# Loading the next batch's k, q and v between the weight tiles, with DMA issues in program order and a later start of its attention

## The chip, the core and the metric

The kernel runs on one core of a Trainium2 chip. The metric is the device time of one execution in microseconds, as the median of several runs. The engines are named as the profile names them: PE is TensorE (matrix products and transpositions), ACT is ScalarE, DVE is VectorE, POOL is GpSimd, and SP is SyncE, which here does nothing but issue DMAs. SPq is SP's instruction queue.

## What is computed

There are 8 batches of 8 heads, 576 positions, a head size of 64, and 32 pack vectors per head. Each batch goes through two attentions, first from the pack vectors to the sequence and then from the sequence to the packed result. A feed-forward layer with a softplus follows.

```
def sm_attn(qq, kk, vv):
    s = scale * qq @ kk.T;  s -= max(s);  a = exp(s)
    return (a / (sum(a) + 1e-09)) @ vv
p_packed = sm_attn(p, k, v)
out      = sm_attn(q, p_packed, p_packed)        # (8, 8, 576, 64)
x = out as (4608, 512)
h = x @ w_in                                     # w_in: 512 x 2048
g = max(h, 0) + log1p(exp(-|h|))
result = g @ w_out                               # w_out: 2048 x 512, float32
```

The two weight matrices arrive as 64-bit floating point numbers. The kernel makes 32-bit numbers of them on the chip, with integer operations.

## The kernel before

**Units.** The feed-forward part of a batch is cut into 16 units f of 128 columns of w_in (rows of w_out). The loop over `units` runs through all of them, batch after batch. Unit f has a first product `gemm1` (tiles `ph`, two halves c of 288 positions, 12 matrix products of 288 columns), the softplus on ACT (absolute value, exponential, logarithm) and DVE (`e`, line 624), and a split of the result into a high and a low part on DVE (`gh`, `gl`, lines 611 and 612). The second product `gemm2_tile` (12 products of 512 columns into four accumulators `acc`) comes two units later (LAG = 2). Two `ph` banks exist for each pair of halves in turn, so the first product of unit f+1 waits until DVE has read `ph` of unit f.

**The factored first product.** The second attention's product with the packed vectors is not formed. `make_m` multiplies the packed vectors (`pt`) with columns of w_in (tiles `psm`, then `mh` and `ml`), and `gemm1` multiplies these with the attention weights `at_h` and `at_l`. In batch 0 one `make_m` serves two units: `psm` number c needs w_in's column tiles 2c and 2c+1, and it stands on PE two units ahead of its use, after the second products of the unit that is then in hand.

**Weight conversion.** `convert` goes through 32 tiles in the order i0, i1, o0, o1, i2, i3, o2, o3 and so on (i for w_in, o for w_out), so tile n = 12 is i6 and n = 24 is i12. For each: a DMA of 512 KB into a tile x (lines 149 to 157; two DMAs for an i tile, one for an o tile), two passes on ACT (`m`, line 196, and `r`, line 200), two on DVE (`t`, lines 202 and 207), and an addition on POOL (line 215). For an i tile the addition writes w_in's columns. For an o tile ACT copies the sum to `wo_h` (line 234) and DVE forms `wo_l` (line 240). From n = 8 on there are two x tiles in turn, so the load of tile n+2 waits until ACT has read tile n. There is one tile `m` in the main loop, so line 196 of tile n+1 waits until DVE has done line 207 of tile n. `conv` is advanced by CONV = 1.6 steps per quarter unit in batch 0.

**The next batch's attention.** `attention(b + 1)` is a generator that runs beside the units of batch b. It is advanced by PACE = 0.56 steps per quarter of a unit, from the batch's first quarter on, and what is left of it is run in unit 15. Its first step transposes k on DVE (`quads`, tiles `T_k`, line 252), and `scores1` multiplies the result with the pack vectors on PE (tiles `ps1`, line 276). q is transposed some steps later (`T_q`). k, q and v of the next batch are issued from within these generators: batch 1's k and v from `attention_first(0)`, and each batch's q from `attention_next` of its own.

**What sets the order.** PE's instructions stand in the order of the program. Those of the other engines, SP's DMA issues among them, are put in order by a scheduler that works with the program's priorities and its own view of durations. Each engine then runs its list strictly in order, so an instruction that waits holds up all that stand behind it. The k and q tiles share two buffers (tag `kq`), v has two of its own.

Of the kernel before, what the change touches and what calls it, by code (L numbers as in the profile page):

```python
# [9 lines left out]
F32 = mybir.dt.float32  # L10
# [16 lines left out]
def pack_attention_then_softplus_ffn(  # L27
# [14 lines left out]
    P = 128  # L42
# [3 lines left out]
    C = S // 2  # L46
    G = H * J // P
    HG = H // G
    NF = DFF // P
    NT = S // P  # L50
    REST = S - NT * P
    LAG = 2
    MC = 512
    Q = 32
    FIRST = 1
    scale = 1.0 / math.sqrt(D)

    const = ctx.enter_context(tc.tile_pool(name="const", bufs=1))
    ld = ctx.enter_context(tc.tile_pool(name="ld", bufs=G))
    cv = ctx.enter_context(tc.tile_pool(name="cv", bufs=1))  # L60
# [56 lines left out]
    def load(nm, b, g):  # L117
        if b >= B:
            return
        src = {"q": q, "k": k, "v": v}[nm][b, g * HG:(g + 1) * HG]  # L120
        if b < FIRST:
            if nm == "v":
                t = ld.tile([NP, HG, SI, D], F32, tag="v", name=f"{nm}_{b}_{g}")
            else:
                o = DFF - (["k", "q"].index(nm) * G + g + 1) * SI * D
                t = w_in_sb[:NP, :, o:o + SI * D].rearrange("x h (s d) -> x h s d", d=D)
            nc.sync.dma_start(
                t.rearrange("x h s d -> x h (s d)"),
                src.rearrange("h (x s) d -> x h (s d)", s=SI),
            )  # L130
        elif nm == "v":
            t = ld.tile([NP, HG, SI, D], F32, tag="v", name=f"{nm}_{b}_{g}")
            nc.sync.dma_start(
                t.rearrange("x h (m c) d -> x (h m) (c d)", c=2),
                src.rearrange("h (m x c) d -> x (h m) (c d)", x=NP, c=2),
            )
        else:
            t = ld.tile([P, HG, C], F32, tag="kq", name=f"{nm}_{b}_{g}")
            by_quad = src.rearrange("h (n x c) (e d) -> c e x (h n) d", x=Q, c=2, d=Q)
            for i in range(P // Q):  # L140
                nc.sync.dma_start(
                    t[i * Q:(i + 1) * Q].rearrange("x h (n d) -> x (h n) d", d=Q),
                    by_quad[i // 2, i % 2],
                )
        loaded[nm, b, g] = t
# [224 lines left out]
    def attention_first(b):  # L370


        a1 = [work.tile([P, S], F32, tag="a1", name=f"a1_{b}_{g}") for g in range(G)]
        pp = [None] * G
        kT, qT = [], []
        kt = turned("k", b, 0)
        for hh in range(HG):
            kT.append(transposed("k", b, 0, hh, kt))
            yield
        for c in range(2):  # L380
            scores1(b, 0, c, kT, a1[0])
        yield
        nm = softmax1_max(b, 0, a1[0])
        kt = turned("k", b, 1)
        kT = [transposed("k", b, 1, 0, kt)]
        yield
        z0 = softmax1_exp(b, 0, a1[0], nm)
        kT.append(transposed("k", b, 1, 1, kt))
        yield
        rs0 = softmax1_sum(b, 0, z0)  # L390
        for hh in range(2, HG):
            kT.append(transposed("k", b, 1, hh, kt))
            yield
        for c in range(2):
            scores1(b, 1, c, kT, a1[1])
        yield
        nm = softmax1_max(b, 1, a1[1])
        a1T = work.tile([NP, SI, P], F32, tag="a1T", name=f"a1T_{b}_0", bufs=1)
        for c in range(2):
            a1_transposed(b, 0, c, a1[0], a1T)  # L400
            yield
            if c == 0:
                z1 = softmax1_exp(b, 1, a1[1], nm)
        rs1 = softmax1_sum(b, 1, z1)
        pp[0] = packed(b, 0, a1T, rs0)
        load("k", b + 1, 0)
        yield
        qt = turned("q", b, 0)
        qT.append(transposed("q", b, 0, 0, qt))
        yield  # L410
        a1T = work.tile([NP, SI, P], F32, tag="a1T", name=f"a1T_{b}_1", bufs=1)
        for c in range(2):
            a1_transposed(b, 1, c, a1[1], a1T)
            yield
        res[b]["pt"].append(packed_transposed(b, 0, pp[0]))
        yield
        qT.append(transposed("q", b, 0, 1, qt))
        yield
        pp[1] = packed(b, 1, a1T, rs1)
        load("k", b + 1, 1)  # L420
        yield
        for hh in range(2, HG):
            qT.append(transposed("q", b, 0, hh, qt))
            yield
        load("v", b + 1, 0)
        a2 = scores2(b, 0, 0, qT)
        a2n = scores2(b, 0, 1, qT)
        yield
        softmax2_exp(b, 0, 0, a2)
        res[b]["pt"].append(packed_transposed(b, 1, pp[1]))  # L430
        yield
        qt = turned("q", b, 1)
        qT = [transposed("q", b, 1, 0, qt)]
        softmax2_div(b, 0, 0, a2)
        a2 = a2n
        yield
        qT.append(transposed("q", b, 1, 1, qt))
        softmax2_exp(b, 0, 1, a2)
        yield
        qT.append(transposed("q", b, 1, 2, qt))  # L440
        yield
        qT.append(transposed("q", b, 1, 3, qt))
        softmax2_div(b, 0, 1, a2)
        yield
        load("v", b + 1, 1)
        a2 = scores2(b, 1, 0, qT)
        a2n = scores2(b, 1, 1, qT)
        yield
        softmax2_exp(b, 1, 0, a2)
        yield  # L450
        softmax2_exp(b, 1, 1, a2n)
        softmax2_div(b, 1, 0, a2)
        yield
        softmax2_div(b, 1, 1, a2n)
        yield

    def attention_next(b):
# [2 lines left out]
        a1 = [work.tile([P, S], F32, tag="a1", name=f"a1_{b}_{g}") for g in range(G)]  # L460
        kT = [quads("k", b, 0)]
        yield
        load("q", b, 0)
        kT.append(quads("k", b, 1))
        yield
        load("q", b, 1)
        yield
        for c in range(2):
            scores1(b, 0, c, kT[0], a1[0])
        yield  # L470
# [55 lines left out]
        yield  # L526
        softmax2_div(b, 1, 1, a2n)
        yield

    def attention(b):  # L530
        return attention_first(b) if b < FIRST else attention_next(b)
# [151 lines left out]
    for f in range(NF):  # L683
        if f % 2 == 0:
            order += [("i", f), ("i", f + 1)]
        order.append(("o", f))
    PACE = 0.56
    CONV = 1.6
    CONV_EARLY = 1.6
    CONV_STEP = 14  # L690
# [16 lines left out]
    due = 0.0  # L707
# [8 lines left out]
    spare.clear()  # L716
    cdue = 0.0
    gs, acc = {}, None
    units = [(b, f) for b in range(B) for f in range(NF)]
    ahead, chain, due = iter(()), iter(()), 0.0  # L720
    for u in range(len(units) + LAG):
# [25 lines left out]
        for t in range(NT):  # L747
            if u >= LAG:
                gemm2_tile(
                    acc[t], gh, gl, f2, slice(t * P, (t + 1) * P), f2 == 0, f2 == NF - 1  # L750
                )
                if f2 == NF - 1:
                    store(acc[t], [(0, b2, t * P, P)], f"{b2}_{t}")
            if u < len(units):
                due += PACE
                while due >= 1:
                    next(ahead, None)
                    due -= 1
                if b == 0:
                    cdue += CONV  # L760
                    while cdue >= 1:
                        next(conv, None)
                        cdue -= 1
            next(chain, None)
# [37 lines left out]
```

## Time and profile before

| | us |
|---|---|
| median of 3 runs (836.68 to 838.5) | 838.15 |
| the profiled execution | 836.29 |
| its span in the trace | 834.5 |
| from batch 0's first unit to batch 1's first unit (52.9 to 215.4) | 162.5 |
| of these, PE busy | 96.67 |
| from there to the end (seven batches of units) | 619.1 |
| of these, PE busy | 613.58 |

The profile is one execution. Busy times of PE include the overlap of the products' pipelined ends. "Idle before" is the time in which an engine's next instruction could not begin, and what it waited for. The granted clock is a share of 2.4 GHz: 1.00 is 2.4 and 0.50 is 1.2.

### The profile page before, as it was taken

To read this page: it belongs to the slowest core of one execution; us is meant where nothing else is said; L and a number is where in the kernel's file an instruction comes from. 1 tells how busy PE (TensorE), PEld (TensorE's weight loads), DVE (VectorE), ACT (ScalarE), POOL (GpSimd) and SP (SyncE) were. 2 spreads that over 40 slices of the span, in tenths; PEclk is the share of its full clock that TensorE was granted. 3 is DMA by queue.
4 is the path that set the end of the run, shared out by engine and by line. 5 is a ranking of instruction groups with operands and counts; after the bars stand their busy time and mean duration, and the time that the engine had idled before them with its cause. 6 is when DMAs were issued, how large, how long until landed. Compare 5 with 4: busy or idle time off the path is not lost.

```text
span 834.5 us, 14191 instructions
## 1 busy us (share of the span) xinstructions
PE 734.6 (88%) x5312; PEld 580.9 (70%) x5312; DVE 543.5 (65%) x1228; ACT 434.1 (52%) x1073; POOL 89.5 (11%) x166
## 2 busy tenths in 40 slices
PE   5636546537999999999999999999999999999997
PEld 3324434426777877788778877787878777888886
DVE  2684557565757785595758665877586756765544
ACT  5643555446665554455655625466546355555550
POOL 1220222132000000000000000000000000000110
PEclk9557788768999999999999999999999999999999
DMA  9781536264153113230523032212321100000002
GB/s 213 211 169 29 136 83 148 77 168 100 36 105 61 29 52 60 67 55 10 108 57 59 1 91 59 57 30 75 62 57 30 51 14 1 1 26 26 1 1 63
DMA packets 168244, 55.96 MB, mean 67 GB/s; under 512 B 134896, under 2 KB 161520, under 8 KB 168176
## 3 DMA queue, kind: packets, MB, share of 16 engines
q1 hardware_dynamic: 167904, 55.00, 29.8%
q8 instruction: 41, 0.67, 0.3%
q14 instruction: 27, 0.22, 0.1%
q10 hardware_dynamic: 272, 0.07, 0.0%
HBM read 45.61 MB, written 9.44 MB: 66 GB/s over the span
## 4 chain that ended last, share of the span: by engine, by line
PE 78%; DVE 9%; DMA 5%; ACT 4%; issue 2%; POOL 2%; SPq 0%; DVEq 0%; POOLq 0%; ACTq 0%
PE acc L635 39%; PE ph L597 25%; PE acc_m L635 4%; PE psm L560 4%; DMA x_o<-in_moe_w_out 2%; PE ps L276 2%; DVE t L207 2%; DMA x_i<-in_moe_w_in 1%; PE psp L319 1%; POOL t L215 1%; DVE t L202 1%; PE psa L309 1%; ACT m L196 1%; DMA out<-o 1%; DVE e L624 1%
## 5 line engine op out<-in xcount | busy, mean ns | idle before, releaser
L624 DVE SCALAR_TENSOR_TENSOR e<-ph,e 128x288 f32<-128x288 f32 x256 | 113.4, 452 | 161.7 <-ACT e L622 161.1
L635 PE MATMUL acc<-wo_h,gh 128*128 128x512 f32 x512 | 208.5, 407 | 0.0
L635 PE MATMUL acc<-wo_l,gh 128*128 128x512 f32 x512 | 201.5, 394 | 0.0
L635 PE MATMUL acc<-wo_h,gl 128*128 128x512 f32 x512 | 201.0, 393 | 0.0
L619 ACT ACTIVATE e<-ph 128x288 f32<-128x288 f32 x256 | 102.9, 403 | 152.8 <-PE ph L597 140.6
L597 PE MATMUL ph<-at_h,mh 128*128 128x288 f32 x512 | 161.0, 314 | 11.1 <-ACT at_h L542 5.9
L597 PE MATMUL ph<-at_l,mh 128*128 128x288 f32 x512 | 155.7, 304 | 12.0 <-DVE at_l L543 12.0
L597 PE MATMUL ph<-at_h,ml 128*128 128x288 f32 x512 | 155.8, 304 | 0.0
L597 PEld LDWEIGHTS ph<-at_h,mh 128*128 128x128 f32 x512 | 100.4, 196 | 47.0 <-issue 16.4
L635 PEld LDWEIGHTS acc<-wo_h,gh 128*128 128x128 f32 x512 | 97.1, 190 | 27.5 <-issue 10.2
L628 POOL COPY rest<-e 128x64 f32<-128x64 f32 x128 | 46.5, 363 | 621.4 <-DVE e L624 592.4
L597 PEld LDWEIGHTS ph<-at_l,mh 128*128 128x128 f32 x512 | 100.7, 197 | 15.5 <-DVE at_l L543 12.4
L635 PEld LDWEIGHTS acc<-wo_h,gl 128*128 128x128 f32 x512 | 96.5, 189 | 21.4
L621 ACT ACTIVATE e<-e 128x288 f32<-128x288 f32 (+1 forms) x240 | 109.2, 455 | 4.0
L622 ACT ACTIVATE e<-e 128x288 f32<-128x288 f32 (+1 forms) x240 | 109.2, 455 | 3.0
L635 PEld LDWEIGHTS acc<-wo_l,gh 128*128 128x128 f32 x512 | 97.1, 190 | 13.3
L597 PEld LDWEIGHTS ph<-at_h,ml 128*128 128x128 f32 x512 | 100.6, 196 | 0.0
L612 DVE TENSOR_TENSOR gl<-e,gh 128x512 fp32r<-128x512 f32 x128 | 87.9, 686 | 6.6 <-DVE gh L611 0.5
L560 PE MATMUL psm<-w_in_sb,pt 64*32 64x512 f32 (+1 forms) x576 | 38.7, 595 | 51.8 <-POOL w_in_sb L215 51.8
L575 ACT CAST mh<-psm 128x512 fp32r<-128x512 f32 (+1 forms) x72 | 35.5, 540 | 64.7 <-PE psm L560 64.7
L576 DVE TENSOR_TENSOR ml<-psm,mh 128x512 fp32r<-128x512 f32 (+1 forms) x72 | 43.0, 627 | 34.5 <-ACT mh L575 34.5
L611 DVE CAST gh<-e 128x512 fp32r<-128x512 f32 x128 | 55.4, 433 | 6.6
(71 smaller groups left out, 706.0 us busy)
## 6 DMA issues: line engine op xcount, KB each, us to landing
v<-in_v SPq DMA_DIRECT2D x16, 576.0 KB, 4.8
x_i<-in_moe_w_in SPq DMA_DIRECT2D x32, 256.0 KB, 4.1
x_o<-in_moe_w_out SPq DMA_DIRECT2D x16, 512.0 KB, 5.2
k<-in_k SPq DMA_DIRECT2D x56, 144.0 KB, 3.1
q<-in_q SPq DMA_DIRECT2D x56, 144.0 KB, 3.2
out<-o SPq DMA_DIRECT2D x21, 256.0 KB, 2.1
out<-o SPq DMA_DIRECT2D x10, 192.0 KB, 2.3
w_in_sb<-in_k SPq DMA_DIRECT2D x2, 576.0 KB, 6.1
```

The source lines that it names most:

```text
L560: nc.tensor.matmul(ps[hh * J:(hh + 1) * J, :n], res["pt"][g][o:o + D, hh * J:(hh + 1) * J], w_in_sb[o:o + D, hh, c * n:(c + 1) * n], start ...
L575: nc.scalar.copy(mh[:, cols], ps[:, :n])
L576: nc.vector.tensor_tensor(ml[:, cols], ps[:, :n], mh[:, cols].bitcast(F32), op=ALU.subtract)
L597: nc.tensor.matmul(ph[:, :C], x[:, ms], y[:, g, cs], start=(i == 0), stop=(i == 3 * G - 1),)
L611: nc.vector.tensor_copy(hi, x)
L612: nc.vector.tensor_tensor(lo, x, hi.bitcast(F32), op=ALU.subtract)
L619: nc.scalar.activation(es[c], hv[c], AF.Abs)
L621: nc.scalar.activation(x, x, AF.Exp, scale=-1.0)
L622: nc.scalar.activation(x, x, AF.Ln, bias=1.0)
L624: nc.vector.scalar_tensor_tensor(es[c], hv[c], 0.0, es[c], op0=ALU.max, op1=ALU.add)
L628: nc.gpsimd.tensor_copy(rest[:, rest_at(b, f), r:r + REST], e[:, NT * P:])
L635: nc.tensor.matmul(acc, x[:, cs], y[:, f, :], start=(first and i == 0), stop=(last and i == 2),)
```

## The change

SP is added to the engines whose instructions stay in program order. Batch 1's six loads leave the generators and go to a generator `loads`, which is advanced once per quarter unit in batch 0. It issues one load every fourth quarter, in the order k0, k1, q0, v0, v1, q1. Batch 1's second k tile no longer takes one of the two `kq` buffers: it is put into the second half of the tile `rest`, which the units fill from f = 9 on. The attention of batch 1 is held for the first AFTER = 10 quarters. `attention_next` gets two steps more ahead of `scores1`, and its q loads (of batches 2 to 7) come two steps later.

```
+    ctx.enter_context(
+        tc.manual_schedule(engines={mybir.EngineType.PE, mybir.EngineType.SP})
+    )
...
-            t = ld.tile([P, HG, C], F32, tag="kq", name=f"{nm}_{b}_{g}")
+            if (nm, b, g) == ("k", FIRST, G - 1):
+                t = rest[:, (NF + LAG) // 2:, :].rearrange("x f j -> x (f j)")
+                t = t.rearrange("x (h n) -> x h n", h=HG)
+            else:
+                t = ld.tile([P, HG, C], F32, tag="kq", name=f"{nm}_{b}_{g}")
...
     (attention_first)
-        load("k", b + 1, 0)
...
-        load("k", b + 1, 1)
...
-        load("v", b + 1, 0)
...
-        load("v", b + 1, 1)
...
     (attention_next)
         kT = [quads("k", b, 0)]
         yield
-        load("q", b, 0)
         kT.append(quads("k", b, 1))
         yield
-        load("q", b, 1)
-        yield
+        yield
+        for g in range(G):
+            if b > FIRST:
+                load("q", b, g)
+            yield
...
+    def loads(b):
+        for nm, g in (("k", 0), ("k", 1), ("q", 0), ("v", 0), ("v", 1), ("q", 1)):
+            load(nm, b, g)
+            for _ in range(4):
+                yield
...
+    AFTER = 10
...
+    early = loads(FIRST)
...
-                due += PACE
+                if b < FIRST:
+                    next(early, None)
+                due += PACE if b >= FIRST or NT * f + t >= AFTER else 0
```

Three places show how the instructions move. In the names the batch comes first: `ph_0_1_1` is batch 0, unit 1, half 1, `ps1_1_0_0` is batch 1's first scores, `e_0_9` is the softplus of unit 9, `m_24` and `r_24` belong to conversion tile 24, and `mh_0_6` is the factor that units 12 and 13 use.

On PE, batch 1's first scores stand before between units 1 and 2:

```order
L597 MATMUL ph_0_1_1_632<-at_l_0_541,mh_0_0_0_534 128x288
L597 MATMUL ph_0_1_1_632<-at_h_0_540,ml_0_0_0_535 128x288
L276 MATMUL ps1_1_0_0_671<-T_k_1_0_574,pT_91 32x288 x4
L276 MATMUL ps1_1_0_1_677<-T_k_1_0_574,pT_91 32x288 x4
L597 MATMUL ph_0_2_0_691<-at_h_0_540,mh_0_1_0_619 128x288
```

After the change they stand among the second products of unit 3:

```order
L608 MATMUL ph_0_5_1_892<-at_h_0_528,ml_0_2_0_744 128x288
L646 MATMUL acc_0_0_679<-wo_h_90,gh_0_3_799 128x512
L646 MATMUL acc_0_0_679<-wo_l_91,gh_0_3_799 128x512
L646 MATMUL acc_0_0_679<-wo_h_90,gl_0_3_800 128x512
L283 MATMUL ps1_1_0_0_914<-T_k_1_0_719,pT_93 32x288 x4
L283 MATMUL ps1_1_0_1_920<-T_k_1_0_719,pT_93 32x288 x4
```

So `scores1` moves by four units, and between units 1 and 2 nothing of batch 1 is left; the second scores (`ps1_1_1`) move from the second products of unit 1 to those of unit 4.

On ACT, ahead of `mh_0_6`, which needs tiles 24 and 25 (i12 and i13), the list before has four conversions in a row behind unit 10:

```order
L200 ACTIVATE r_22_1196<-x_o10_1089 128x512
L355 ACTIVATE a2_1_1_0_1440<-a2_1_1_0_1440 128x288
L200 ACTIVATE r_23_1234<-x_o11_1119 128x512
L355 ACTIVATE a2_1_1_1_1447<-a2_1_1_1_1447 128x288
L196 ACTIVATE m_23_1232<-x_o11_1119 128x512
L234 CAST wo_h_88<-t_22_1198 128x512
L234 CAST wo_h_88<-t_23_1236 128x512
L196 ACTIVATE m_24_1282<-x_i12_1200 128x512
L200 ACTIVATE r_24_1284<-x_i12_1200 128x512
L196 ACTIVATE m_25_1352<-x_i13_1238 128x512
L200 ACTIVATE r_25_1354<-x_i13_1238 128x512
L575 CAST mh_0_6_0_1488<-psm_0_6_0_1478 128x256
```

After the change the same stretch reads:

```order
L207 ACTIVATE r_24_1177<-x_i12_1107 128x512
L241 CAST wo_h_90<-t_23_1134 128x512
L633 ACTIVATE e_0_9_1262<-e_0_9_1262 128x576
L317 COPY a1T_1_1_1277<-psa_1_1_0_1278 96x384
L317 COPY a1T_1_1_1277<-psa_1_1_1_1300 96x384
L203 ACTIVATE m_25_1283<-x_i13_1136 128x512
L207 ACTIVATE r_25_1285<-x_i13_1136 128x512
L630 ACTIVATE e_0_10_1346<-ph_0_10_0_1332 128x288
L630 ACTIVATE e_0_10_1346<-ph_0_10_1_1339 128x288
L632 ACTIVATE e_0_10_1346<-e_0_10_1346 128x576
L633 ACTIVATE e_0_10_1346<-e_0_10_1346 128x576
L586 CAST mh_0_6_0_1443<-psm_0_6_0_1433 128x256
```

Tiles 24 and 25 have moved from behind unit 10 to within unit 9 and ahead of unit 10.

On ACT, ahead of `mh_0_7`, which needs tiles 28 and 29 (i14 and i15), two conversions stand around the end of unit 12 before:

```order
L622 ACTIVATE e_0_11_1508<-e_0_11_1508 128x576
L619 ACTIVATE e_0_12_1574<-ph_0_12_0_1560 128x288
L619 ACTIVATE e_0_12_1574<-ph_0_12_1_1567 128x288
L621 ACTIVATE e_0_12_1574<-e_0_12_1574 128x576
L196 ACTIVATE m_28_1460<-x_i14_1379 128x512
L200 ACTIVATE r_28_1462<-x_i14_1379 128x512
L622 ACTIVATE e_0_12_1574<-e_0_12_1574 128x576
L196 ACTIVATE m_29_1526<-x_i15_1404 128x512
L200 ACTIVATE r_29_1528<-x_i15_1404 128x512
L575 CAST mh_0_7_0_1628<-psm_0_7_0_1618 128x256
```

After the change, with unit 12's logarithm and the first instruction of tile 26 just ahead of this piece:

```order
L207 ACTIVATE r_26_1307<-x_o12_1181 128x512
L241 CAST wo_h_90<-t_26_1309 128x512
L203 ACTIVATE m_27_1323<-x_o13_1289 128x512
L207 ACTIVATE r_27_1325<-x_o13_1289 128x512
L241 CAST wo_h_90<-t_27_1327 128x512
L203 ACTIVATE m_28_1399<-x_i14_1311 128x512
L207 ACTIVATE r_28_1401<-x_i14_1311 128x512
L203 ACTIVATE m_29_1474<-x_i15_1329 128x512
L207 ACTIVATE r_29_1476<-x_i15_1329 128x512
L207 ACTIVATE r_30_1497<-x_o14_1405 128x512
L203 ACTIVATE m_30_1495<-x_o14_1405 128x512
L586 CAST mh_0_7_0_1586<-psm_0_7_0_1576 128x256
```

Here tiles 26 and 27 have moved from ahead of unit 11 to behind unit 12, so four conversions and the first of the next ones stand in a row.

## Rows read from the trace of the kernel before

**Rows 1.** The page: PE's busy tenths and its granted clock in 40 slices of the span (20.9 us each), and two rows of the DMA issues (KB each, median us from issue to landing).

```profile
PE   5636546537999999999999999999999999999997
...
PEclk9557788768999999999999999999999999999999
...
x_i<-in_moe_w_in SPq DMA_DIRECT2D x32, 256.0 KB, 4.1
...
q<-in_q SPq DMA_DIRECT2D x56, 144.0 KB, 3.2
```

**Rows 2.** Busy time of each engine in two stretches, from batch 0's first unit to batch 1's, and from there to the end. Columns: stretch, length, busy time and count of PE, PEld, DVE, ACT, POOL, then the granted clock, the DMA share and GB/s.

```profile
52.90:215.40 162.50, 96.67 (x670) 73.68 (x670) 97.88 (x202) 79.80 (x157) 35.80 (x38) 0.76 0.45 103
215.40:834.50 619.10, 613.58 (x4397) 491.33 (x4396) 414.52 (x956) 324.79 (x852) 41.13 (x113) 1.00 0.21 45
```

**Rows 3.** PE's waits in the first of these stretches: who waited, for whom, us in total, times, longest.

```profile
PE psm L560 <- POOL w_in_sb L215: 51.8, 5, 15.8
...
PE ps L276 <- DVE T_k L252: 8.9, 2, 4.8
PE ph L597 <- DVE e L624: 5.1, 3, 2.7
```

**Rows 4.** The same view from 215.5 us to the end, where this is the only row.

```profile
PE acc_m L635 <- DVE gl_m L612: 1.0, 3, 0.6
```

**Rows 5.** PE in order of time: start, duration, what, and in brackets the idle time before it and its releaser. The rows with `psm` are numbers 3 to 7 of batch 0.

```profile
61.29 0.45 PE L597 MATMUL ph<-at_h,ml 128*128 128x288 f32 x1
...
66.49 1.77 PE L276 MATMUL ps<-T_k,pT 64*32 64x288 f32 x16 [4.75 <-DVE T_k L252]
...
76.27 0.29 PE L597 MATMUL ph<-at_h,ml 128*128 128x288 f32 x1
...
81.39 1.77 PE L276 MATMUL ps<-T_k,pT 64*32 64x288 f32 x16 [4.13 <-DVE T_k L252]
...
100.79 1.11 PE L560 MATMUL psm<-w_in_sb,pt 64*32 64x256 f32 x16 [9.48 <-POOL w_in_sb L215]
...
126.34 1.11 PE L560 MATMUL psm<-w_in_sb,pt 64*32 64x256 f32 x16 [12.13 <-POOL w_in_sb L215]
...
149.18 1.11 PE L560 MATMUL psm<-w_in_sb,pt 64*32 64x256 f32 x16 [9.97 <-POOL w_in_sb L215]
...
177.23 1.11 PE L560 MATMUL psm<-w_in_sb,pt 64*32 64x256 f32 x16 [15.85 <-POOL w_in_sb L215]
...
197.14 0.74 PE L560 MATMUL psm<-w_in_sb,pt 64*32 64x256 f32 x16 [4.41 <-POOL w_in_sb L215]
```

**Rows 6.** PE in order of time again: the first product of unit 9 begins behind a wait, the second products of unit 7 follow, and after them the first product of unit 10.

```profile
150.22 0.61 PE L597 MATMUL ph<-at_h,mh 128*128 128x288 f32 x1
...
153.25 0.39 PE L635 MATMUL acc<-wo_h,gh 128*128 128x512 f32 x1
...
156.02 0.30 PE L597 MATMUL ph<-at_h,mh 128*128 128x288 f32 x1
...
157.61 0.39 PE L635 MATMUL acc<-wo_h,gh 128*128 128x512 f32 x1
```

**Rows 7.** ACT in order of time: two i tiles in turn, one softplus, and an o tile from its first pass to its copy.

```profile
93.09 0.67 ACT L196 ACTIVATE m<-x_i 128x512 f32<-128x512 f32 x1
...
96.97 0.66 ACT L196 ACTIVATE m<-x_i 128x512 f32<-128x512 f32 x1 [2.66 <-DVE t L207]
...
105.11 0.41 ACT L619 ACTIVATE e<-ph 128x288 f32<-128x288 f32 x1 [1.03 <-PE ph L597]
105.56 0.69 ACT L621 ACTIVATE e<-e 128x576 f32<-128x576 f32 x1
106.28 0.68 ACT L622 ACTIVATE e<-e 128x576 f32<-128x576 f32 x1
...
178.65 0.69 ACT L196 ACTIVATE m<-x_o 128x512 f32<-128x512 f32 x1
...
182.07 0.62 ACT L234 CAST wo_h<-t 128x512 fp32r<-128x512 f32 x1 [0.71 <-POOL t L215]
```

**Rows 8.** DVE in order of time: the softplus sums of units 1 and 3, a low part, a transposition of q, and the first pass over a conversion tile, once beside POOL's addition of the tile before it and once alone.

```profile
63.64 0.82 DVE L624 SCALAR_TENSOR_TENSOR e<-ph,e 128x288 f32<-128x288 f32 x2 [3.46 <-ACT e L622]
...
78.55 0.82 DVE L624 SCALAR_TENSOR_TENSOR e<-ph,e 128x288 f32<-128x288 f32 x2 [2.46 <-ACT e L622]
...
79.87 0.69 DVE L612 TENSOR_TENSOR gl<-e,gh 128x512 fp32r<-128x512 f32 x1
...
94.43 1.43 DVE L252 STREAM_TRANSPOSE T_q<-q 128x576 f32<-128x576 f32 x2
...
97.67 0.96 DVE L202 TENSOR_SCALAR t<-m 128x512 int32<-128x512 int32 x1 [0.78 <-ACT m L196]
...
121.30 0.42 DVE L202 TENSOR_SCALAR t<-m 128x512 int32<-128x512 int32 x1
```

**Rows 9.** POOL in order of time: the addition for tile i7.

```profile
99.48 1.26 POOL L215 TENSOR_TENSOR w_in_sb<-t,r 128x512 int32<-128x512 int32 x1 [1.14 <-issue]
```

**Rows 10.** SP's waits in the whole span: an x load that waits for ACT's reading of the tile two before it.

```profile
SPq L154 <- ACT r L200: 73.3, 14, 15.2
```

**Rows 11.** SP in order of time: the four loads of one q tile, and one batch's output stores.

```profile
262.76 2.79 SPq L141 DMA_DIRECT2D q<-in_q  x4
...
304.83 5.99 SPq L656 DMA_DIRECT2D out<-o  x5
```

## Prediction

> **What bounds the kernel now.** I read the page's slices first [rows 1]: from the eleventh slice on PE is busy nine tenths and more at full clock, and in the first ten it is busy about half the time at a clock between 0.5 and 0.9. So I cut the span there [rows 2]. From batch 1's first unit on, 613.58 of 619.1 us are PE work at clock 1.00, and all that PE waits for is 1.0 us [rows 4]. Nothing but less PE work could shorten that part, and the change removes none. The stretch of batch 0's units is 162.5 us long and holds 96.67 us of PE work, so 65.8 us are waits. They are three kinds [rows 3]: 51.8 us in five waits of `make_m` for POOL's last addition to w_in, 8.9 us in two waits of batch 1's scores for the transposed k, and 5.1 us of first products that wait for DVE to free `ph`. Each is a place on PE [rows 5]. POOL is busy 35.8 of these 162.5 us, ACT 79.8, DVE 97.9, the DMAs 0.45: no engine is full. The waits are latency, one conversion after the other, and what decides is the place of each conversion in ACT's and DVE's lists. SP's longest wait says the same: 73.3 us of x loads that wait until ACT has read the tile two before [rows 10].
>
> **The change part by part.** I walked through the new lists of PE, ACT, DVE, POOL and SP from 52.9 us on, with durations from the rows. Four durations recur. From a unit's last first product to the end of its logarithm are 2.0 us (0.41, 0.69 and 0.68 start one behind the other, 105.11 to 106.96) [rows 7]. DVE's sum and split take 2.0 us (78.55 to 80.56) [rows 8]. From an i tile's first ACT pass to the `make_m` that waits for it are 3.8 us (96.97 to 100.79), and from an o tile's to the end of its copy 4.0 us (178.65 to 182.69) [rows 5, 7]. Against these stand the second products of one unit, 2.8 us (153.25 to 156.02) [rows 6]; what exceeds them is a wait.
>
> A. *Scores of batch 1, four units later.* Both waits for `T_k` go, -8.9. Late next is the softplus. Unit 1's last product ends at 61.74 and DVE's sum at 64.46: PE waits 2.7 us there for `ph`. Unit 3's sum ends 2.8 us after its products (76.56 to 79.37), and now o5's copy and i6's two passes (0.6 + 1.2) stand before its logarithm: 4.6 less 2.8, 1.8 us [rows 5, 7, 8]. Net -4.4. The scores' own PE time is moved, not removed.
>
> B. *The five waits of `make_m`*, now 9.5, 12.1, 10.0, 15.9 and 4.4 [rows 5]. SP issues in program order and o4 is read right behind i5, so the conversions stand one or two tiles earlier against the units.
> Number 3 (i7): i7 stands behind unit 4's logarithm, its load long there. 2.0, then on DVE sum, split and a transposition of k (2.0 and 1.4), then mask to `make_m` 2.6 (97.67 to 100.79 is 3.1 with a contested mask of 0.96; alone it is 0.42) [rows 5, 8]: 8.0 less 2.8, about 5.
> Number 4 (i8, i9): behind unit 6 come o7 and its copy, and o7's mask stands behind a row maximum and a transposition of q. 2.0 + 2.0 + 4.0, then i8 until its `m` is free (between 1.8 and the 3.9 from 93.09 to 96.97; I take 2.4, since in the new list only `wo_l` stands between) and 3.8 for i9: 14.2, less 2.8 and the scores (1.77 at half clock, so 0.9): about 11.
> Number 5 (i10, i11): 2.0, DVE's sum, split and transposition with a small scaling 3.9, i10's DVE passes 1.1, i11 3.8: 10.8, less 2.8 and a packed product (taken as long as the scores): 7.
> Number 6 (i12, i13): both stand ahead of unit 10 on ACT, so they are done during unit 9's and 10's products. I take 1; the bounds are 0 and 8.
> Number 7 (i14, i15) gets worse: four conversions behind unit 12. 2.0, o12 4.0, then o13's passes free the slot that i15's load needs: 1.2, two issues at the 0.7 of a q load, 4.1 to land [rows 1, 11], then 3.8 for i15: 16.5 less 2.8, about 14.
> Sum 38 against 51.8: -13.8.
>
> C. *What is late next.* The softplus waits grow where conversions now stand inside a softplus (units 3, 7, 9, 13): 5.1 to about 7, +2. o4's passes ahead of the first units' softplus: +0.7. Batch 1's attention has 28 steps by unit 15 and is finished only there, so DVE's last divisions, transpositions and `at_l` come behind unit 14's softplus and just before batch 1's first unit: the trace of before shows no such end, the bounds are 0 and 8 (some twenty DVE passes of 0.4 us), I take +3, since unit 13's second products cover the first half. Together +5.7.
>
> D. *Clock.* Behind a wait PE runs at 1.2 GHz for about one unit's first product: 3.03 us against 1.59 [rows 6], so some 1.6 us each. Before, seven such restarts follow waits of 2.7 us and more (six of rows 5, without that at 66.49 in the slow beginning, and the longest softplus wait of rows 3); then four. -5.
>
> **Nothing from SP itself.** The new order puts k, q and v loads between the x loads. Those of batch 1 wait for nothing that is not long done: k1 has `rest`, q1 takes k0's buffer after its transposition, v's buffers are free since the first attention. The moved x loads wait for their slots anyway [rows 10]. If that cover were gone, four loads of 0.7 us would stand in front of a weight tile, 2.8 us at each of three tiles.
>
> Sum: -4.4 - 13.8 + 5.7 - 5 = -17.5 us. The profiled execution took 836.29 (span 834.5), 1.9 below the median of the runs, 838.15. So 818.8 on its own footing and 820.6 on the median's: I say **819**.
>
> **One rule against it.** A mask on DVE beside POOL's addition took 0.96 us, alone 0.42 [rows 8]: 0.5 us in the second tile of each pair. The Trainium skill ("SBUF — State Buffer", Who interferes with whom) says that DVE and GpSimd share a port pair as an exclusive lock, so that the one that comes second "fully blocks" for the whole instruction. Taken at its worst, a full addition of 1.26 us [rows 9] instead of 0.5 in each of four paths, that adds 3 us, and the sum would be 822. The trace shows the smaller price, and I keep it.
>
> **The rivals.**
> *Less gain, 826 to 835.* The two x tiles still bind. If o11's chain slips by a few us, i13's load comes late and number 6 waits 8 to 14 us again; the sum is then -9.5 to -3.5. For it: 73.3 us of slot waits [rows 10], and my walk has only about 2 us of slack at that place. Against it: i13 is now two units ahead.
> *More gain, 803 to 811.* The conversions that run ahead at unit 9 also shorten numbers 4 and 5 by 4 us each, and the end of the attention costs nothing (-3): -25 to -28, with the clock's share up to -33. Against it: all three stand behind work that the lists show.
> *Slower, above 840.* In program order q's loads of batches 2 to 7 stand behind the output stores of the batch before, where the scheduler had put them ahead. DVE's transposition of q then holds up the softplus behind it, and PE loses time in each of six batches, where it now waits for nothing [rows 4]. It decides from 3.2 us per batch on (17.5 and 1.7 over six). Against it: the loads are issued at the end of unit 1 and transposed behind unit 5, some four units of 5.5 us (619.1 over 112) later, 22 us; stores 6.0, four issues 2.8 and 3.2 to land are 12 [rows 1, 11]. So 10 us of cover.
> *Nothing.* ACT and DVE are still in a scheduler's order; if waits only change places in batch 0 (number 7 does), it is 836.5 to 839.8.
>
> **How the numbers follow.** My forecast, 811 to 826: 0.56. Less gain: 0.19. More gain: 0.09. Within 0.2% (1.7 us, about what a measurement can tell): 0.06. Slower: 0.10, the slower rival and slips that I did not see. So faster 0.84, same 0.06, slower 0.10. For eight in ten the range takes in the forecast, most of less gain and some of more: 805 to 833. Its width comes from number 6 (0 to 8), number 7, the attention's end (0 to 8) and the clock.
>
> **What would show it.** Batch 1's scores should show no wait for `T_k`. `make_m` number 6 should wait under 3 us, number 7 over 10, numbers 3 to 5 together about 23 against 31.6. The stretch from batch 0's first unit to batch 1's should fall from 162.5 to about 145, at a mean clock above 0.76, and the rest should stay at 619. It is wrong if that rest grows, with PE waiting for DVE's `e` in units 4 to 6 of each batch, or if number 6 still waits 10 us and more.

## The result and the profile after

The changed kernel takes 814.85 us (four runs, 814.35 to 815.41) against 837.94 of the kernel before (four runs beside them). The ratio is 0.973, with a 95% interval of 0.971 to 0.974. The forecast was 819, in a range of 805 to 833. The profiled execution took 814.35 (span 812.4), 21.9 less than that of before.

The busy time of each engine in the two stretches of [rows 2], for the kernel after, with the same columns:

```profile
52.80:193.40 140.60, 94.20 (x669) 72.01 (x669) 93.71 (x200) 78.66 (x155) 35.74 (x38) 0.79 0.50 119
193.40:812.40 619.00, 614.37 (x4396) 492.80 (x4396) 419.34 (x958) 324.51 (x853) 40.46 (x113) 1.00 0.23 47
```

Batch 0's stage fell from 162.5 to 140.6 us, and all the gain is there: the rest is 619.0, as before. In the stage PE's own work is 2.5 us less, so 19.4 of the 21.9 us are waits. PE's waits in this stage (as [rows 3]):

```profile
PE psm L571 <- POOL w_in_sb L222: 36.5, 4, 13.3
...
PE ph L608 <- DVE e L635: 8.9, 5, 2.4
PE psm L571 <- DVE a L350: 0.7, 1, 0.7
```

The T_k line of [rows 3] is gone, and `make_m` waits 37.2 us where it waited 51.8. PE in order of time (as [rows 5]); the rows with `psm` are numbers 3 to 7, those with `T_k` batch 1's scores, and the last is the first product of batch 1:

```profile
59.08 0.61 PE L608 MATMUL ph<-at_h,mh 128*128 128x288 f32 x1 [2.23 <-DVE e L635]
64.75 0.61 PE L608 MATMUL ph<-at_h,mh 128*128 128x288 f32 x1 [2.42 <-DVE e L635]
77.72 0.40 PE L608 MATMUL ph<-at_h,mh 128*128 128x288 f32 x1 [1.50 <-DVE e L635]
87.48 1.11 PE L571 MATMUL psm<-w_in_sb,pt 64*32 64x256 f32 x16 [5.16 <-POOL w_in_sb L222]
92.79 0.71 PE L283 MATMUL ps<-T_k,pT 64*32 64x288 f32 x16
99.36 0.72 PE L283 MATMUL ps<-T_k,pT 64*32 64x288 f32 x16
112.30 1.11 PE L571 MATMUL psm<-w_in_sb,pt 64*32 64x256 f32 x16 [11.32 <-POOL w_in_sb L222]
121.65 0.40 PE L608 MATMUL ph<-at_h,mh 128*128 128x288 f32 x1 [1.67 <-DVE e L635]
134.04 1.20 PE L571 MATMUL psm<-w_in_sb,pt 64*32 64x256 f32 x16 [6.76 <-POOL w_in_sb L222]
149.69 1.42 PE L571 MATMUL psm<-w_in_sb,pt 64*32 64x256 f32 x16 [0.67 <-DVE a L350]
173.49 1.11 PE L571 MATMUL psm<-w_in_sb,pt 64*32 64x256 f32 x16 [13.28 <-POOL w_in_sb L222]
182.56 0.40 PE L608 MATMUL ph<-at_h,mh 128*128 128x288 f32 x1 [1.10 <-DVE e L635]
193.44 0.40 PE L608 MATMUL ph<-at_h,mh 128*128 128x288 f32 x1 [0.16 <-DVE e L635]
```

Numbers 3 to 7 now wait 5.2, 11.3, 6.8, 0.7 and 13.3 us, where the walk through the lists had 5, 11, 7, 1 and 14. Both scores stand without a bracket and take 0.7 us at full clock instead of 1.77. The last row shows that the end of batch 1's attention costs next to nothing.

### The profile page after: what moved, and what is told of

It reads as the page before. It is cut to its first block, busy times and chain, and to the rows that moved or that the text cites. A ratio compares the mean times of both kernels' runs of the same rounds, so it can differ in the third digit from the quotient of the medians.

```text
span 812.4 us, 14187 instructions
## 1 busy us (share of the span) xinstructions
PE 731.1 (90%) x5312; PEld 580.2 (71%) x5312; DVE 544.1 (67%) x1228; ACT 433.2 (53%) x1073; POOL 88.8 (11%) x166
## 4 chain that ended last, share of the span: by engine, by line
PE 82%; DVE 7%; DMA 3%; ACT 3%; POOL 2%; issue 1%; SPq 0%; POOLq 0%; DVEq 0%; ACTq 0%
PE acc L646 41%; PE ph L608 26%; PE acc_m L646 5%; PE psm L571 4%; PE ps L283 2%; DMA x_o<-in_moe_w_out 2%; DVE t L214 2%; POOL t L222 1%; PE psp L326 1%; DVE t L209 1%; PE psa L316 1%; DMA x_i<-in_moe_w_in 1%; DVE wo_l L247 1%; DVE e L635 1%; ACT m L203 1%
## 5 line engine op out<-in xcount | busy, mean ns | idle before, releaser
L608 PE MATMUL ph<-at_l,mh 128*128 128x288 f32 x512 | 155.4, 304 | 12.1 <-DVE at_l L554 12.0
```

The costliest lines, as they stand in the source:

```text
L608: nc.tensor.matmul(ph[:, :C], x[:, ms], y[:, g, cs], start=(i == 0), stop=(i == 3 * G - 1),)
```

## The experiments

"Stage" is the time from batch 0's first product to batch 1's first product in the profiled execution, "rest" is from there to the end of the span. Waits are those of `make_m` numbers 3 to 7, in us. The ratio is to the kernel before, with its 95% interval.

| kernel | median us | ratio | stage | rest | waits of make_m |
|---|---|---|---|---|---|
| before | 837.94 | 1 | 162.5 | 619.1 | 9.5, 12.1, 10.0, 15.9, 4.4 |
| after | 814.85 | 0.973 (0.971 to 0.974) | 140.6 | 619.0 | 5.2, 11.3, 6.8, 0.7, 13.3 |
| order_alone | 848.96 | 1.012 (1.007 to 1.016) | 160.1 | 627.8 | 9.6, 12.1, 8.5, 16.2, 3.1 |
| sp_scheduled | 821.4 | 0.981 (0.979 to 0.982) | 145.3 | 621.7 | 4.7, 11.3, 6.5, 1.3, 12.5 |
| begin_2 | 821.95 | 0.981 (0.979 to 0.982) | 149.6 | 618.4 | 2.0, 10.4, 11.2, 11.5, 4.7 |
| later_alone | 832.8 | 0.995 (0.993 to 0.997) | 157.8 | 620.2 | 15.4, 4.6, 13.3, 8.3, 16.1 |
| q_at_once | 825.5 | 0.985 (0.981 to 0.989) | 141.5 | 630.5 | 4.7, 11.3, 6.5, 0.7, 13.3 |
| loads_back | 816.08 | 0.974 (0.971 to 0.977) | 141.4 | 618.9 | 15.4, 0.3, 12.0, 0.7, 13.3 |
| two_m | 812.68 | 0.970 (0.969 to 0.972) | 139.2 | 620.2 | 5.3, 10.9, 6.2, 0.7, 13.3 |
| conv_ahead | 803.81 | 0.959 (0.958 to 0.961) | 125.8 | 622.3 | 1.6 in all |
| later_two_steps | 825.81 | 0.987 (0.986 to 0.989) | 146.6 | 623.8 | 15.4, 7.7, 13.1, 1.3, 11.4 |
| steps_later_only | 833.73 | 0.996 (0.995 to 0.998) | 160.5 | 618.5 | 15.4, 4.8, 13.3, 11.1, 15.5 |
| ahead_10 | 814.74 | 0.974 (0.972 to 0.975) | 135.4 | 624.5 | 10.4 in all |
| ahead_loads_close | 799.88 | 0.956 (0.955 to 0.958) | 121.3 | 624.9 | 14.8 in all |

**First four: which part pays?** The theory was that the moved loads let o4, and with it every later tile, come earlier; the rivals were the held attention and SP's order.

order_alone, the kernel before with SP in program order:

```
+    ctx.enter_context(
+        tc.manual_schedule(engines={mybir.EngineType.PE, mybir.EngineType.SP})
+    )
```

> The kernel before with one edit, SP's instructions in program order; loads, places and the attention's begin as before. Theory A (conversions come one or two tiles earlier because batch 1's k, q and v no longer stand ahead of o4's load): SP still issues k_1_0, k_1_1 and v_1_0 ahead of o4, ACT's list ahead of mh_0_3 to mh_0_6 is that of before, so make_m waits near 9.5, 12.1, 10, 15.9 and about 3 (i14 now ahead of unit 12), T_k waits near 8.9; 835 to 838 us. Rival B (the later begin is what pays): 838. Rival C (the order of the issues is what pays): about 818.

The waits of the stage are those expected, but the time missed the range by 11 us: the rest grew by 8.7 us, which no theory had. SP in order of time at the end of batch 1, and PE's row behind it:

```profile
301.13 1.69 SPq L659 DMA_DIRECT2D out<-o  x2
302.87 4.08 SPq L144 DMA_DIRECT2D q<-in_q  x4
307.05 1.91 SPq L659 DMA_DIRECT2D out<-o  x3
```

```profile
321.32 0.79 PE L638 MATMUL acc<-wo_h,gh 128*128 128x512 f32 x1 [2.08 <-DVE o_m L655]
```

q's load of the next batch stands between two output stores, and the three stores behind it start only after its 4 us. No copy of an accumulator waits long for that: DVE idles 0.8 us for a store in all. What changed is the order of DVE's list. DVE at this batch end, first in the kernel before, then in order_alone:

```profile
318.87 0.69 DVE L652 COPY o_m<-acc_m 128x512 f32<-128x512 f32 x1 [2.12 <-PE acc_m L635]
321.34 0.46 DVE L624 SCALAR_TENSOR_TENSOR e<-ph,e 128x288 f32<-128x288 f32 x1 [1.78 <-ACT e L622]
```

```profile
318.09 0.46 DVE L627 SCALAR_TENSOR_TENSOR e<-ph,e 128x288 f32<-128x288 f32 x1 [4.59 <-ACT e L625]
...
320.58 0.68 DVE L655 COPY o_m<-acc_m 128x512 f32<-128x512 f32 x1
```

Before, the copy of `acc_m` to `o_m` stands ahead of the next softplus sum, and PE does not wait for it. In order_alone it stands behind the sums and the split: PE's last product into `acc_m` ends at 315.6, but DVE waits 4.6 us for ACT with the copy behind, and PE waits 2.1 us for `o_m`. It is the same at three batch ends, 6.2 us in all. PE's own work in the rest is 2.1 us more (615.7 against 613.6), part of it at half clock behind this first wait. The scheduler orders DVE's list, and SP's order is all that was changed; why this moved the copy is not shown. Four executions took 841.7 to 850.8 us, and the profiled one is the quickest; what the others lost beyond it stays open.

sp_scheduled, the changed kernel without it:

```
-    ctx.enter_context(
-        tc.manual_schedule(engines={mybir.EngineType.PE, mybir.EngineType.SP})
-    )
```

> The changed kernel with one edit undone: SP's issues are put in order by the scheduler again. Theory A: SP's list up to i13 keeps nearly the new order and ACT's list is the new one up to mh_0_5; only i13 now stands behind unit 10, so make_m number 6 waits about 3 us instead of 0.7; 815 to 819 us. Rival B: 815. Rival C: 830 or more.

The waits of `make_m` came nearly as expected, yet the time is 2.4 us above the range and 6.5 us above the changed kernel. The span of the profiled execution is 8.3 us longer: 0.9 ahead of the stage, 4.7 in the stage, where PE's own work is 98.2 us instead of 94.2, and 2.7 in the rest, of which 2.0 are one wait for `o`. The order of SP is worth something, but not the whole.

begin_2, the changed kernel with the attention held for 2 quarters:

```
-    AFTER = 10
+    AFTER = 2
```

> The changed kernel with batch 1's attention held for 2 quarters instead of 10 (with 0, its second k tile would be read before its load is issued). Theory A: no wait for T_k comes back, since k0 and k1 are loaded early and scores1 has two steps more; make_m numbers 3 to 5 as in the changed kernel (5, 11, 7), number 6 about 10 (o11, i12 and i13 behind unit 10), number 7 about 3 (i14 ahead of unit 12): about 36 us in all, 812 to 818 us. Rival B: the T_k waits of 8.9 us come back and 823 us or more. Rival C: 815.

Missed by 4 us: one wait for `T_k` did come back (3.1 us), and number 5 is 11.2 instead of 7. The held attention is worth 7 us here.

later_alone, the kernel before with the attention held:

```
+    AFTER = 10
...
-                due += PACE
+                due += PACE if b >= FIRST or NT * f + t >= AFTER else 0
```

> The kernel before with one edit, batch 1's attention held for 10 quarters; its loads, their places, the two steps and SP's order as before. Theory A: the T_k waits of 8.9 us go, but o4 still stands behind batch 1's k and v, and now o4, o5, i6 and i7 all stand behind unit 4: make_m number 3 waits about 16 us (was 9.5), number 4 about 5, number 5 about 16 (four tiles behind unit 8), number 6 about 7, number 7 about 14: nearly 58 in all against 51.8; 830 to 838 us. Rival B: 822 us or less. Rival C: 838.

As the theory had it: the two T_k waits go, and four tiles each behind units 4, 8 and 12 take most of that back, 57.7 us for `make_m` instead of 51.8. So neither the order nor the held attention brings more than 0.5% alone. That the moved loads bring the rest was not yet shown.

**Second four.** q_at_once, the changed kernel with q's loads of batches 2 to 7 where they were:

```
         kT = [quads("k", b, 0)]
         yield
+        if b > FIRST:
+            load("q", b, 0)
         kT.append(quads("k", b, 1))
         yield
+        if b > FIRST:
+            load("q", b, 1)
         yield
-        for g in range(G):
-            if b > FIRST:
-                load("q", b, g)
-            yield
+        if b == FIRST:
+            yield
+            yield
```

> The changed kernel, but from batch 2 on attention_next has its old steps again: two fewer ahead of scores1, and q's loads two steps earlier, so that in SP's program order they stand between the output stores and not behind them. Theory A (a load that waits for its buffer holds up the stores behind it, and these hold the two x tiles that the accumulators are emptied into): batch 0's stage stays near 140.6 us and the rest grows from 619 to about 627, with PE waiting about 2 us at each of three batch ends for DVE's copy of the accumulator: about 823 us. Rival: SP's order there is of no matter, the rest stays at 619 and the time at 815.

The stage stays, the rest grows by 11.5 us to 630.5. PE's waits in the rest:

```profile
PE acc L649 <- DVE o_m L666: 6.2, 3, 2.1
PE acc_m L649 <- DVE gl_m L626: 1.8, 3, 1.4
```

The size fits the theory, but not its reason: at all three batch ends DVE's copy to `o_m` again stands behind the next softplus sums, as in order_alone, and DVE idles only 1.2 us for a store. So program order on SP costs nothing in the rest only because the change also issues q's loads later; there the copy stands ahead of the sums, as before.

loads_back, the changed kernel with batch 1's loads where they were (k's, v's and q's; one of the four in `attention_first` stands here for all):

```
-            if (nm, b, g) == ("k", FIRST, G - 1):
-                t = rest[:, (NF + LAG) // 2:, :].rearrange("x f j -> x (f j)")
...
+        load("k", b + 1, 0)
...
         for g in range(G):
-            if b > FIRST:
-                load("q", b, g)
+            load("q", b, g)
             yield
...
-                if b < FIRST:
-                    next(early, None)
```

> The changed kernel with the loads alone undone: batch 1's k, q and v are issued from within the attentions as before, k's second tile in a kq buffer; SP's program order, the held attention and the two steps stay. Theory A: SP issues k_1_0, k_1_1 and v_1_0 ahead of o4 again; the conversions come late as in later_alone: make_m number 3 about 15 us (o4, o5, i6, i7 behind unit 4), number 4 about 2 (none behind unit 6), number 5 about 11, number 6 about 2, number 7 about 14; 44 us in all against 36.5 of the changed kernel, stage about 149, 823 us. Rival B (the held attention is what pays): 815. Rival C (SP's order is what pays): 815.

Here my theory fell. Without the moved loads the kernel takes 816.08, and its interval covers that of the changed kernel. PE in order of time, numbers 3 to 7:

```profile
95.52 1.11 PE L570 MATMUL psm<-w_in_sb,pt 64*32 64x256 f32 x16 [15.42 <-POOL w_in_sb L218]
...
110.32 0.85 PE L570 MATMUL psm<-w_in_sb,pt 64*32 64x256 f32 x16 [0.33 <-ACT a L288]
...
134.03 1.21 PE L570 MATMUL psm<-w_in_sb,pt 64*32 64x256 f32 x16 [12.01 <-POOL w_in_sb L218]
...
150.15 1.42 PE L570 MATMUL psm<-w_in_sb,pt 64*32 64x256 f32 x16 [0.67 <-DVE a L346]
...
173.93 1.11 PE L570 MATMUL psm<-w_in_sb,pt 64*32 64x256 f32 x16 [13.29 <-POOL w_in_sb L218]
```

o4 stands behind batch 1's k and v again, and number 3 waits 15.4 instead of 5.2. But the tiles converted during that wait are missing later: number 4 waits 0.3 instead of 11.3. The five waits sum to 41.7 us instead of 37.2; PE's own work in the stage is 2.2 us less, the other waits are shorter too, and the stage is 141.4 us against 140.6.

two_m, the changed kernel with a second place for m (part of `first`; `by` gives both sides the same shape):

```
+            if not spare and n % 2 and order[n] != ("i", NF - 1) and n < len(order) - 2:
+                m = w_in_sb[:, :, DFF - P:]
+                nc.scalar.activation(m, by(hi.bitcast(F32)), AF.Copy, scale=2.0**-112)
+            else:
                 m = pool.tile([P, CN], F32, tag=tm, name=f"m_{n}", bufs=LAG + 1 if pool is work else 1)
```

> The changed kernel with a second place for m in the main loop: odd tiles write it into the columns of w_in that tile i15 will fill (i15 itself and the last two tiles use the old place). ACT's list is nearly that of the changed kernel. If an i tile's first pass waits for DVE to be done with the tile before (theory A: a step of 3.9 us per tile, 1.2 of it passes), then each make_m with two tiles in a row behind its unit gains about 2.6 us: number 4 from 11.3 to 7 to 9, number 5 from 6.8 to about 4.2, number 7 from 13.3 to about 10.7; 805 to 808 us. Rival (the x loads bind): 813 to 815.

The rival is right on the size: 2 us (0.3 below its range), of which 1.4 are in the stage, and number 7 is unchanged. ACT in order of time ahead of number 7 shows why:

```profile
160.12 0.62 ACT L247 CAST wo_h<-t 128x512 fp32r<-128x512 f32 x1 [2.88 <-POOL t L228]
...
163.99 0.62 ACT L247 CAST wo_h<-t 128x512 fp32r<-128x512 f32 x1 [2.12 <-POOL t L228]
...
166.71 0.66 ACT L209 ACTIVATE m<-x_i 128x512 f32<-128x512 f32 x1 [0.97 <-DMA x_i<-in_moe_w_in]
```

An o tile holds ACT with its copy, which waits for POOL's addition, and the next tile's passes stand behind it in ACT's list. The place for m is not what binds; the last i tile waits for its load.

conv_ahead, the changed kernel with two numbers altered:

```
-    AFTER = 10
-    CONV = 1.6
+    AFTER = 4
+    CONV = 3.2
```

> The changed kernel with conversions advanced by 3.2 steps per quarter unit instead of 1.6, and the attention held for 4 quarters instead of 10. In ACT's list no tile that make_m numbers 3 to 7 need stands behind the unit before them. Theory A: the five waits of make_m fall from 36.5 us to under 5; what is late next is the softplus, with six tiles in a row ahead of unit 8's (6 times 3.9 us, less what PE is ahead), two ahead of unit 10's and two behind unit 12's: waits for DVE's e grow from 9 to 25 or 35; 800 to 813 us. Rival (the conversions are bound by their own chain of 3.9 us per tile, wherever they stand): 815 or more.

The time fits, at 803.81, by other waits than those forecast. PE's waits in the stage, and SP in order of time:

```profile
PE psp L326 <- DMA v<-in_v: 13.8, 1, 13.8
...
PE ph L608 <- DVE e L635: 8.7, 7, 2.4
PE ps L283 <- DVE T_q L259: 4.3, 1, 4.3
PE ps L283 <- DVE T_k L259: 4.1, 1, 4.1
...
PE psm L571 <- POOL w_in_sb L222: 0.6, 1, 0.6
```

```profile
106.57 5.33 SPq L161 DMA_DIRECT2D x_i<-in_moe_w_in  x4
112.02 0.52 SPq L136 DMA_DIRECT2D v<-in_v  x1
```

`make_m` hardly waits, and the softplus did not get worse. What is late next is v: its load stands on SP behind x loads that wait for their tiles.

**Last four: the parts that were left, and the way on.** later_two_steps, on top of later_alone:

```
         load("q", b, 1)
         yield
+        yield
+        yield
         for c in range(2):
```

> later_alone with one more part of the change: the two steps ahead of scores1 (for batch 1 and all later ones). Loads and the scheduler's SP order as in the kernel before. After loads_back (816 us without the moved loads) three parts are left to tell apart: the held attention, the two steps, SP's program order. Theory D (what counts is where each tile stands against the units in ACT's list, whichever part put it there): the list has o4, o5, i6, i7 behind unit 4, i9 alone behind unit 6, four tiles behind unit 8, i13 alone behind unit 10, three behind unit 12: make_m waits near 15, 4, 13, 3 and 11, 46 in all; 820 to 827 us. Rival (SP's order is what pays): 832. Rival (the two steps are what pays): 816.

steps_later_only, on top of loads_back:

```
         kT = [quads("k", b, 0)]
         yield
+        if b == FIRST:
+            load("q", b, 0)
         kT.append(quads("k", b, 1))
         yield
+        if b == FIRST:
+            load("q", b, 1)
         yield
         for g in range(G):
-            load("q", b, g)
-            yield
+            if b > FIRST:
+                load("q", b, g)
+                yield
```

> loads_back with the two steps taken out for batch 1 alone (its q loads are issued two steps earlier; batches 2 to 7 keep the later q loads): SP's program order and the held attention stay. Theory D: SP issues q_1_0 and q_1_1 ahead of i9 and o8 instead of behind o8, and ACT's list has the counts of later_alone again: make_m waits near 15, 4.5, 13, 8 and 16, stage near 158, the rest 619: 830 to 833 us. Rival (SP's order is what pays): 816 to 820.

Both fit theory D: 825.81 within its range, 833.73 at 0.7 above it. The attention held and the loads where they were, the stage is 157.8 with neither the steps nor SP's order, 146.6 with the steps alone, 160.5 with the order alone, and 141.4 with both. So the steps of batch 1 bring 11 to 19 us of the stage, and SP's order 5 on top of them and nothing without. Batch 1's q loads come two steps later in the last of these kernels alone; what that place brings is not told apart from the rest.

ahead_10, the changed kernel with one number altered:

```
-    CONV = 1.6
+    CONV = 3.2
```

> The changed kernel with one number altered: conversions advanced by 3.2 steps per quarter unit instead of 1.6; the attention is held for 10 quarters as in the changed kernel. Theory D: no tile behind units 4, 10 and 12, three behind unit 6 and four behind unit 8 (with two more of which make_m does not need): waits near 0, 11, 13, 0 and 0, 24 against 36.5; the wait for v (13.8 us in conv_ahead) shrinks, since the attention is 1.5 units later; 803 to 812 us. Rival (the pace is of no matter, the chain through ACT, DVE and POOL binds): 815.

A miss: 814.74, no better than the changed kernel. The waits of `make_m` fell to 10.4, but the wait for v did not shrink. It now stands just ahead of `make_m` number 5, the second row of PE here:

```profile
131.73 1.51 PE L326 MATMUL psp<-v,a1T 96*32 96x64 f32 x48 [13.08 <-DMA v<-in_v]
...
134.75 1.11 PE L571 MATMUL psm<-w_in_sb,pt 64*32 64x256 f32 x16
```

Four tiles stand behind unit 8 here, as expected, and number 5 waits for nothing: they are converted while PE waits for v. One wait hides the other. The rest is 5.5 us longer than after, with 3.6 us of waits for `e` in it.

ahead_loads_close, the changed kernel with that number and closer loads:

```
-            for _ in range(4):
+        order = (("k", 0), ("k", 1), ("q", 0), ("v", 0), ("v", 1), ("q", 1))
+        for (nm, g), gap in zip(order, (1, 1, 1, 1, 16, 4)):
+            load(nm, b, g)
+            for _ in range(gap):
...
-    CONV = 1.6
+    CONV = 3.2
```

> As ahead_10, and batch 1's first five loads are issued in five quarters in a row instead of one in four, so that on SP both v loads stand ahead of o7 and not behind i11 and i13; the second q load stays at its quarter. Theory D: one tile or none behind units 6 to 12, i6 and i7 behind unit 4: make_m waits near 7, 3, 0, 0 and 0; no wait for v (13.8 us in conv_ahead) and none for T_k (4.1); softplus waits of 8 to 14 us remain; stage 110 to 117, 787 to 796 us. Rival (the chain of one conversion after the other binds as soon as make_m no longer waits): 801 or more.

799.88, the fastest of all, 15 us below the changed kernel, though 4 above the range given. The wait for v is gone. The two stretches, and PE's waits in the first:

```profile
53.14:174.44 121.30, 94.25 (x669) 70.97 (x669) 91.24 (x194) 77.39 (x155) 36.65 (x38) 0.85 0.58 138
174.44:799.30 624.86, 616.83 (x4396) 493.95 (x4396) 422.77 (x964) 324.70 (x853) 41.34 (x113) 1.00 0.23 47
```

```profile
PE psm L572 <- POOL w_in_sb L222: 10.3, 2, 7.6
PE ph L609 <- DVE e L636: 7.0, 5, 2.4
PE psm L572 <- DVE pp L334: 2.3, 1, 2.3
PE psm L572 <- DVE a L350: 2.2, 1, 2.2
PE ps L283 <- DVE T_q L259: 1.6, 1, 1.6
```

PE's work is as after, 94 us, and the stage is 19 us shorter; 5.9 of these come back in the rest, where the end of batch 1's attention is now late for the first units (4.0 us of waits for `e` and `at_h`). PE still waits 10.3 us for conversions. The rival had 801 or more, 1.1 us above the time; whether the conversions' own chain binds at 121 us stays open.

## Why the prediction held, step by step

The sum had -17.5 us, measured were -21.9. What was named as its signs came: number 6 waits 0.7 us (under 3), number 7 13.3 (over 10), numbers 3 to 5 together 23.2 (about 23), the mean clock of the stage is 0.79 (above 0.76), the rest stays at 619.0. The stage came out at 140.6 instead of about 145. Two terms were mis-sized, in opposite directions, so that part of the close fit is luck.

*A, the scores.* -8.9, and 2.4 and 1.5 us of softplus waits take their place (forecast 2.7 and 1.8): -5.0 against -4.4.

*B, the waits of make_m.* 37.2 against a forecast of 38, each of the five within 1 us: -14.6 against -13.8. Number 6, on which the rival with less gain rested, waits 0.7. Number 7 is worse than before, as said.

*C, what is late next: the term that was mis-sized most.* It had +5.7, and about +0.6 came. The start is as forecast (2.23 less 1.54, +0.7). The other softplus waits did not grow but fell, from 3.6 to 2.8. The attention's end, taken at +3 with bounds of 0 and 8, costs 0.16 us of waiting and 0.5 us in the unit behind it, whose first product takes 2.2 us (193.44 to 195.60) instead of 1.7 before (215.37 to 217.06). DVE in order of time there:

```profile
192.92 0.82 DVE L635 SCALAR_TENSOR_TENSOR e<-ph,e 128x288 f32<-128x288 f32 x2
...
194.05 0.42 DVE L554 TENSOR_TENSOR at_l<-aT,at_h 128x288 fp32r<-128x288 f32 x1
...
194.72 0.46 DVE L554 TENSOR_TENSOR at_l<-aT,at_h 128x288 fp32r<-128x288 f32 x1
```

The last `at_l` end at 194.47 and 195.18, behind the 193.44 at which batch 1's unit begins: its first products need only the first half's tiles, and the others come just in time. The cover is thin: in ahead_loads_close, with the stage at 121 us, the rest grows by 5.9 us, 4.0 of them waits there for `e` and `at_h`.

*D, the clock: the other term mis-sized.* -5 was forecast. PE's own work fell by 2.5 us, and 2.1 of these are the two scores that run at full clock (1.77 to 0.71 and 0.72). The count of restarts came true, seven before and four after. But a restart costs 3.03 less 1.59, so 1.4 us and not 1.6, and the four after last longer than the seven before: by the starts of the first and second products, an estimate, some 10 us were lost to half clock behind waits before, and some 8 after. `make_m`'s own products took 0.6 us more (8.66 instead of 8.03).

*Nothing from SP itself.* Right for the changed kernel: in the rest there is 0.2 us of waiting. The slower rival was looked for on the wrong side. q's loads later than before did no harm. Program order on SP with q's loads where they were cost 9 to 12 us of the rest, in order_alone and q_at_once, and 6.2 us of that in each are waits for DVE's copy to `o_m`, which stands behind the next softplus there. The two steps more in `attention_next`, which the prediction treated as mere delay, avoid just that.

*The reason given for B* was that SP issues in program order and that o4 is read right behind i5. The first half is wrong: with SP's order alone o4 still stands behind batch 1's k and v, and the waits are those of before. The second half is true, comes from the moved loads, and does not matter in the sum: loads_back gives number 3 its wait back and takes it from number 4. What the waits follow, in before, after and the nine other kernels that have all five in the table, is the count of tiles that stand in ACT's list behind the unit ahead of a `make_m`, up to the last that it needs: four wait 12 to 16 us, three 10 to 12.5, two 6 to 11, one 1 to 8, none under 1. Two of the other three kernels show the limits of this: in ahead_10 four tiles cost nothing behind the wait for v, and in ahead_loads_close number 4 waits 2.7 us with none. The counts for numbers 3 to 7 are 2, 4, 2, 4, 1 before and in order_alone, 4, 1, 4, 2, 4 in later_alone, 4, 0, 3, 0, 4 in loads_back and 1, 3, 2, 0, 4 after. By the lists, the held attention and the steps of batch 1 change them most: q's loads and the attention's passes no longer stand ahead of i9 and i13. How much each part would bring in another order of the lists stays open: the parts do not add up (order alone nothing in the stage, on top of the steps 5 us).

## What to carry to other kernels

When engines run fixed lists, count what stands between the step that frees an engine and the step that waits for it; a change is worth what it does to these counts, and its parts must be tried together and alone, since moved waits turn up two places further. In a queue of DMA issues in program order, a load that waits for its buffer holds up the loads behind it, as the x loads held up v's in conv_ahead, so a load belongs ahead of those that must wait. And a new order on one engine can change the list that a scheduler makes for another: here the place of DVE's copy to `o_m`, 6.2 us of waits. Read every list anew, not only the one that was edited. A wait that is taken away shows the next one: here v's load took 13 of the 27 us that `make_m` gave up, until it was moved too.

## What was unexpected in the hardware

A mask on DVE beside POOL's addition does not run slower, it waits. POOL and DVE in order of time in the kernel after, an addition and the mask beside it:

```profile
108.55 1.28 POOL L222 TENSOR_TENSOR w_in_sb<-t,r 128x512 int32<-128x512 int32 x1 [2.58 <-DVE t L214]
```

```profile
107.26 0.42 DVE L209 TENSOR_SCALAR t<-m 128x512 int32<-128x512 int32 x1
109.19 0.93 DVE L209 TENSOR_SCALAR t<-m 128x512 int32<-128x512 int32 x1 [0.78 <-ACT m L203]
```

The addition ends at 109.83 and the mask at 110.12, 0.29 us later; in all seven such pairs of this stage the difference is 0.28 to 0.30, whether the mask shows 0.77 or 0.93. The Trainium skill ("SBUF — State Buffer", Who interferes with whom) says that DVE in a two-port mode and GpSimd share a port pair that the first to issue holds for its whole instruction, while the other is blocked. The trace agrees with the blocking, but the mask needs only 0.29 us behind the addition, not the 0.42 that it takes alone. So the 0.5 us that the prediction took per tile follows what was left of the addition when the mask came (0.64 us here, of which the mask shows 0.51), and is not a share of a slower rate. By this reading it would come near the addition's 1.26 us only if both began at once, which no row here shows.
